# Two mixers after an attention stage on one core: normalisation issued earlier, transposes spread over units, five conversion steps instead of four

## The chip, the cores and the metric

The kernel runs on one core of a Trainium2 chip. The metric is the device time of one execution in microseconds (us). Engines are named as in the profile: PE is the matrix engine, DVE, ACT and POOL the vector, scalar and general engines, SP the one whose queue issues nearly all transfers (DMA).

## What is computed

The reference is a chain of three stages on a batch of 2, 768 positions and 512 channels. The first is attention with a window and block summaries, the second a mixer over tokens and channels, the third a normalised channel mixer. Cut to the last two, which matter here:

```
xt = x.transpose(0, 2, 1)
h = np.maximum(xt @ w_tok1, 0.0) @ w_tok2
u = x + h.transpose(0, 2, 1)
h2 = np.maximum(u @ w_ch1, 0.0) @ w_ch2
x = u + h2
...
mu = np.mean(x, axis=-1, keepdims=True)
var = np.mean((x - mu) ** 2, axis=-1, keepdims=True)
xn = (x - mu) / np.sqrt(var + 1e-06) * g_ln
ch = np.maximum(xn @ w_ch1, 0.0) @ w_ch2
return (x + ch).astype(np.float32)
```

The weights of both mixers arrive as 64-bit floats, the activations as 32-bit ones.

## The kernel before

Every product is made of three matmuls on pairs (high part, low part) of 32-bit numbers (`mm3`, L273 to L277). The activation `u` stays on the chip, 12 tiles of 128 positions by 512 channels; groups `g` 0 to 3 have three tiles each.

**Conversion of weights.** The 62 halves (128 by 512 each) of the weights are read as two 32-bit words per number, decoded on ACT (L115) and DVE (L129 to L137), and split into high and low part, on ACT (`split_hi`, `sp` or `slot`) and then DVE (`split_lo`). Halves 0 to 29 stay on the chip in `slot` tiles. Halves 30 to 61 are weights of the second mixer: they, and sums of their quarters (`sums`, tiles `sa`, `sb`, `sps`), are written back to DRAM (`w1s`, `w2s`) through two spill buffers `sp`, and are read again into a ring of 12 places as the second mixer needs them (`load_w1`, `load_w2`). The generator `conversion` (L141) cuts this work into steps: a step is about one DVE instruction with the ACT instruction and the transfers that belong to it. `convert_all(n)` issues n steps.

**First mixer.** After attention, 48 units each make one `g3` product and, one unit later, its `g4` accumulation (loop L925 to L972). Behind each unit stands `convert_all(4)` (L972). From unit 39 on the eight steps of `prep_x(0)` are issued between them, one a unit.

**prep_x.** `prep_x(s)` (L575) makes the operands of half `s` of the second mixer: eight steps, each for one 128-channel piece of one group. A step transposes three normalised 128 by 128 blocks on PE (tile `tx`, L585); then ACT evacuates them with the gain (`f`, L589), and ACT and DVE make and split the sums of pieces that the scheme of seven products needs (`split`, L569; T1 to T4). Its last act is to issue the normalisation of the next step (`normalize`, L549: three ACT instructions into the one tile `xn`). `start` runs a step up to its `yield`, the transposes; `finish` runs the rest.

**Second mixer.** 16 units (`unit`, L681), eight for each half `s`. A unit makes seven products of six matmuls (tile `m`, k = 0 to 6), each in one of two result banks of PSUM, which `tx` uses too; DVE adds them up (L686), except that ACT copies the first (tile `sm`, L696), and ACT and DVE make the relu pairs `ah`, `al` (L677, L678). Between the products stand the accumulations `acc_x` of the unit before (`second`, L733), three matmuls each, 12 a unit. After each product `step(k)` (L984) issues two or three conversion steps. In units 1 and 2, behind odd k, it also issues a step of the statistics of groups 2 and 3 (`norm_stats`, queued in `bg`, L993); what is left of them is issued at the end of unit 2 (L996). `prep_x(1)` follows at the ends of units 2 to 5, two of its steps at each (L999 to L1006).

**What sets the order.** PE's order in the second mixer is the one in which the code is written, ACT's from unit 10 of the first mixer on (manual schedule). DVE's and SP's orders are set by the scheduler when the program is built. Each engine takes its instructions in order.

Of the kernel before, what the change touches and what calls it, by code (L numbers as in the profile page):

```python
# [43 lines left out]
NP = F2 // 2  # L44
# [12 lines left out]
class Kern:  # L57
# [517 lines left out]
    def prep_x(self, s):  # L575
        nc = self.nc
        seq = [(e, half, i) for e in range(2) for half, i in ((0, 0), (0, 1), (1, 1), (1, 0))]
        self.normalize(2 * s + seq[0][2], seq[0][0] + 2 * seq[0][1])
        f, t = {}, {}
        for n, (e, half, i) in enumerate(seq):  # L580
            g, cc = 2 * s + i, e + 2 * half
            xn = self.xn.pop((g, cc))
            ps = self.ps_mm.tile([P, 512], F32, tag="mm", name=f"tx_{g}_{cc}")
            for j in range(GT):
                nc.tensor.transpose(ps[:, j * P : j * P + P], xn[:, j], self.ident)  # L585
            yield
            name = f"B{half + 1}{i + 1}"
            x = self.tmp.tile([P, GN], F32, tag="f", bufs=3, name=f"f{s}_{e}_{name}")
            nc.scalar.activation(x, ps[:, :GN], AF.Copy, scale=self.gt[:, cc : cc + 1])  # L589
            f[name] = x  # L590
            new = lambda k: self.tmp.tile([P, GN], F32, tag="t", bufs=2, name=f"t{s}_{e}_{k}")
            if name == "B12":
                t["T1"] = new("T1")
                nc.vector.tensor_tensor(t["T1"], x, f["B11"], op=ALU.subtract)
                self.split(s, "T1", e, t["T1"])
            else:
                self.split(s, name, e, x)
            if name == "B22":
                t["T3"], t["T2"] = new("T3"), new("T2")
                nc.vector.tensor_tensor(t["T3"], x, f["B12"], op=ALU.subtract)  # L600
                nc.vector.tensor_tensor(t["T2"], t["T3"], f["B11"], op=ALU.add)
                self.split(s, "T3", e, t["T3"])
                self.split(s, "T2", e, t["T2"])
            if name == "B21":
                t["T4"] = new("T4")
                nc.vector.tensor_tensor(t["T4"], x, t["T2"], op=ALU.subtract)
                self.split(s, "T4", e, t["T4"])
            if n + 1 < len(seq):
                e, half, i = seq[n + 1]
                self.normalize(2 * s + i, e + 2 * half)  # L610
            else:
                self.ready_xt.add(("x", s))
            yield

# [208 lines left out]
    def run(self):  # L823
# [100 lines left out]
        later = deque()  # L924
        for n, (s, f, g) in enumerate(units):  # L925
# [27 lines left out]
            if xctx is not None and not self.bg and not self.evacs:  # L953
# [15 lines left out]
                    {k: (at(f), 0) for f, k in enumerate(names)},  # L969
                    {k: (t, 0) for k, t in zip(names, flat + [at(f) for f in range(9, 12)])},  # L970
                ]
            self.convert_all(4)  # L972
        while later or self.bg or self.evacs:
            if later:
                self.bg.append(later.popleft())
# [6 lines left out]
        for n in range(2 * NP):  # L982

            def step(k):  # L984
                if n == 0 and k == 0:
                    for r in range(9, RING):
                        self.load_w1(r)
                self.convert_all(2 + k % 2)
                if n in (1, 2) and k % 2:
                    self.start(1)  # L990
                    self.finish()

            if n == 1:  # L993
                self.bg += [self.norm_stats(2)] * (GT + 1) + [self.norm_stats(3)] * (GT + 1)
            pending = self.unit(n, pending, step)
            while 0 < n < 3 and n == 2 and self.bg:  # L996
                self.start(1)
                self.finish()
            if n == 2:  # L999
                later += [self.prep_x(1)] * 8  # L1000
            if 2 <= n < NP - 1:
                for _ in range(2):
                    if later:
                        self.bg.append(later.popleft())
                        self.start(1)
                        self.finish()  # L1006
        while pending:
            pending.popleft()()

# [85 lines left out]
```

## Time and profile before

| what | us |
|---|---|
| runs (three): median, lowest, highest | 615.59, 613.78, 619.37 |
| the profiled execution's own time | 616.25 |
| its span, first to last instruction | 614.2 |
| PE busy | 572.8 |
| DVE busy | 413.2 |
| ACT busy | 257.9 |

The profile is of one execution; its times are us from the start of the span. A row of a timeline gives start, duration, engine, line, operation, tiles written and read, and in brackets the idle time of the engine before it with what ended it. Names in the profile leave out buffer numbers. Attention ends at about 105 us, the first mixer at 322, where unit 0 of the second begins.

### The profile page before, as it was taken

The numbers are of one execution on the slowest core, as the hardware profiler recorded it, in microseconds if no ns is written. First come the engines' busy times: TensorE is split into PE (matmuls) and PEld (weight loads), VectorE is DVE, ScalarE is ACT, GpSimd is POOL, SyncE is SP. The second block draws the span as 40 slices with busy tenths as digits, with TensorE's granted clock in tenths as the row PEclk, the third lists the DMA queues.
The fourth block names the chain that finished last, engine by engine and source line by source line (L and its number), as shares of the span: only waits on it lengthen the run. The fifth ranks groups of instructions, "written<-read, shape, count | busy, mean of one in ns | idle before, by whom it ended". The sixth has DMA issues, their size and how long they took to land.

```text
span 614.2 us, 9748 instructions
## 1 busy us (share of the span) xinstructions
PE 572.8 (93%) x3483; PEld 493.2 (80%) x3488; DVE 413.2 (67%) x992; ACT 257.9 (42%) x559; POOL 45.0 (7%) x78
## 2 busy tenths in 40 slices
PE   7777999999999999999998985798799999999997
PEld 3455778799998989998887874687689998899986
DVE  4699988992577986855798986876643543333334
ACT  4889887440334343325872335445411111111110
POOL 1565621000000000000000000000000000000000
PEclk9999999999999999999999996988999999999999
DMA  8999820442134354854579997875745776666412
GB/s 273 332 298 312 240 83 1 137 167 74 53 119 137 137 202 166 288 190 165 193 252 319 321 352 259 277 268 184 265 138 187 227 240 187 187 188 189 138 34 104
DMA packets 51206, 121.07 MB, mean 197 GB/s; under 512 B 5075, under 2 KB 11475, under 8 KB 51158
## 3 DMA queue, kind: packets, MB, share of 16 engines
q1 hardware_dynamic: 51152, 120.43, 60.3%
q8 instruction: 28, 0.46, 0.3%
q14 instruction: 20, 0.16, 0.1%
q10 hardware_dynamic: 6, 0.02, 0.0%
HBM read 94.21 MB, written 26.21 MB: 196 GB/s over the span
## 4 chain that ended last, share of the span: by engine, by line
PE 71%; DVE 11%; DMA 11%; ACT 4%; issue 2%; SPq 0%; ACTq 0%; DVEq 0%
PE acc_x L275 6%; PE acc_x L276 6%; PE acc_x L277 6%; PE m L275 5%; PE m L276 5%; PE m L277 5%; DMA stage<-in_wts_dram 3%; DMA w1s<-sps 3%; DMA V<-in_v_dram 2%; PE g L275 1%; DVE dec L133 1%; DMA VT<-in_vt_dram 1%; PE g L277 1%; PE g L276 1%; DVE dec L137 1%
## 5 line engine op out<-in xcount | busy, mean ns | idle before, releaser
L276 PE MATMUL acc_x<-slot,ah 128*128 128x512 f32 x192 | 77.0, 401 | 0.0
L275 PE MATMUL acc_x<-slot,ah 128*128 128x512 f32 x192 | 76.8, 400 | 0.0
L277 PE MATMUL acc_x<-slot,al 128*128 128x512 f32 x192 | 76.7, 400 | 0.0
L677 ACT ACTIVATE ah<-sm 128x384 fp32r<-128x384 f32 x32 | 16.7, 523 | 118.3 <-DVE sm L686 118.3
L275 PE MATMUL m<-slot,slot 128*128 128x384 f32 x126 | 45.0, 357 | 1.8 <-ACT sm L696 1.8
L137 DVE SCALAR_TENSOR_TENSOR dec<-stage,dec 128x512 uint32<-128x512 uint32 x62 | 44.1, 712 | 0.8
L115 ACT ACTIVATE dec<-stage 128x512 f32<-128x512 f32 x62 | 41.6, 675 | 5.9 <-DMA stage<-in_wts_dram 5.8
L133 DVE SCALAR_TENSOR_TENSOR dec<-stage,dec 128x512 uint32<-128x512 uint32 x62 | 43.4, 700 | 0.9
L276 PE MATMUL m<-slot,slot 128*128 128x384 f32 x126 | 44.0, 349 | 0.0
L277 PE MATMUL m<-slot,slot 128*128 128x384 f32 x126 | 43.9, 348 | 0.0
L277 PEld LDWEIGHTS acc_x<-slot,al 128*128 128x128 f32 x192 | 37.0, 193 | 8.4
L276 PEld LDWEIGHTS acc_x<-slot,ah 128*128 128x128 f32 x192 | 37.0, 193 | 4.2
L275 PEld LDWEIGHTS acc_x<-slot,ah 128*128 128x128 f32 x192 | 37.0, 193 | 3.9
L391 ACT ACTIVATE pr<-sn,mn 128x120 f32<-128x120 f32 x96 | 30.6, 386 | 6.6 <-DVE mn L381 6.3
L686 DVE TENSOR_TENSOR um<-m,sm 128x384 f32<-128x384 f32 x16 | 8.9, 557 | 30.7 <-PE m L277 30.7
L275 PEld LDWEIGHTS m<-slot,slot 128*128 128x128 f32 x126 | 24.8, 197 | 5.6 <-ACT sm L696 2.6
L131 DVE TENSOR_SCALAR dec<-dec 128x512 uint32<-128x512 uint32 x62 | 27.8, 449 | 0.6
L129 DVE TENSOR_SCALAR dec<-dec 128x512 f32<-128x512 f32 x62 | 26.3, 427 | 1.7 <-ACT dec L115 1.7
L678 DVE SCALAR_TENSOR_TENSOR al<-sm,ah 128x384 fp32r<-128x384 f32 x32 | 17.9, 558 | 13.9 <-ACT ah L677 13.9
L585 PE MATMUL tx<-ident,xn 128*128 128x128 f32 x48 | 12.1, 327 | 16.1 <-ACT xn L554 15.9
L276 PEld LDWEIGHTS m<-slot,slot 128*128 128x128 f32 x126 | 24.8, 197 | 2.2
L361 PE MATMUL scores<-K,Q 64*64 64x120 f32 x384 | 15.4, 275 | 10.2 <-DVE mn L381 7.5
(1392 smaller groups left out, 1486.2 us busy)
## 6 DMA issues: line engine op xcount, KB each, us to landing
stage<-in_wts_dram SPq DMA_DIRECT2D x62, 512.0 KB, 3.6
slot<-w1s SPq DMA_DIRECT2D x94, 256.0 KB, 3.4
slot<-w2s SPq DMA_DIRECT2D x32, 512.0 KB, 4.6
w1s<-sps SPq DMA_DIRECT2D x16, 512.0 KB, 3.8
w2s<-sp SPq DMA_DIRECT2D x16, 512.0 KB, 4.3
V<-in_v_dram SPq DMA_DIRECT2D x16, 306.0 KB, 7.6
extra<-w1s SPq DMA_DIRECT2D x18, 256.0 KB, 3.9
w1s<-sp SPq DMA_DIRECT2D x8, 512.0 KB, 5.2
```

Source lines behind the costliest of these rows:

```text
L115: nc.scalar.activation(m, self.raw[n][:, :, 1].bitcast(F32), AF.Abs)
L129: nc.vector.tensor_scalar(m, m, MAG_LO, MAG_HI, op0=ALU.max, op1=ALU.min)
L131: nc.vector.tensor_scalar(mi, mi, 3, 0x3FFFFFF8, op0=ALU.logical_shift_left, op1=ALU.bitwise_and)
L133: nc.vector.scalar_tensor_tensor(mi, t[:, :, 1], 0xC0000000, mi, op0=ALU.bitwise_and, op1=ALU.bitwise_or)
L137: nc.vector.scalar_tensor_tensor(mi, t[:, :, 0], 29, mi, op0=ALU.logical_shift_right, op1=ALU.bitwise_or)
L275: nc.tensor.matmul(out, lhs[0], rhs[0], start=first, stop=False)
L276: nc.tensor.matmul(out, lhs[0], rhs[1], start=False, stop=False)
L277: nc.tensor.matmul(out, lhs[1], rhs[0], start=False, stop=last)
L361: nc.tensor.matmul(ps[cols, j, e, :NK], Q[rows, 64 * w : 64 * w + 64], K.rearrange("p v c -> p (v c)")[rows, a : a + NK], start=True, stop ...
L391: nc.scalar.activation(pr[:, u], sn[:, u], AF.Exp, bias=mn[:, u : u + 1], scale=-1.0)
L677: nc.scalar.activation(ah, x, AF.Relu)
L678: nc.vector.scalar_tensor_tensor(al, x, 0.0, f32(ah), op0=ALU.max, op1=ALU.subtract)
```

## The change

Three things. In `prep_x` the normalisation of the next step is issued directly behind the evacuation `f`, ahead of the sums and splits. In the second mixer the statistics are all issued in unit 1, one step behind each product and two behind the last, and the eight steps of `prep_x(1)` are issued inside units 2 to 5, behind the products k = 1 and k = 5, instead of in pairs at the units' ends. And the first mixer issues five conversion steps behind each unit instead of four.

```
@@ prep_x @@
             nc.scalar.activation(x, ps[:, :GN], AF.Copy, scale=self.gt[:, cc : cc + 1])
             f[name] = x
+            if n + 1 < len(seq):
+                ne, nh, ni = seq[n + 1]
+                self.normalize(2 * s + ni, ne + 2 * nh)
             new = lambda k: self.tmp.tile([P, GN], F32, tag="t", bufs=2, name=f"t{s}_{e}_{k}")
...
-            if n + 1 < len(seq):
-                e, half, i = seq[n + 1]
-                self.normalize(2 * s + i, e + 2 * half)
-            else:
+            if n + 1 == len(seq):
                 self.ready_xt.add(("x", s))
             yield
@@ run @@
-            self.convert_all(4)
+            self.convert_all(5)
         while later or self.bg or self.evacs:
...
                 self.convert_all(2 + k % 2)
-                if n in (1, 2) and k % 2:
-                    self.start(1)
-                    self.finish()
+                if n == 1 or n in range(2, 6) and k in (1, 5):
+                    for _ in range(2 if (n, k) == (1, 6) else 1):
+                        self.start(1)
+                        self.finish()
 
             if n == 1:
                 self.bg += [self.norm_stats(2)] * (GT + 1) + [self.norm_stats(3)] * (GT + 1)
+            if n == 2:
+                self.bg += [self.prep_x(1)] * 8
             pending = self.unit(n, pending, step)
-            while 0 < n < 3 and n == 2 and self.bg:
-                self.start(1)
-                self.finish()
-            if n == 2:
-                later += [self.prep_x(1)] * 8
-            if 2 <= n < NP - 1:
-                for _ in range(2):
-                    if later:
-                        self.bg.append(later.popleft())
-                        self.start(1)
-                        self.finish()
```

PE's order at the end of unit 2 before the change. In the names the number behind `m` is the product k, the next the unit; behind `tx` stand the group and the channel piece.

```order
L277 MATMUL m6_2_4193<-slot9_1627,extra_1832 128x384
L275 MATMUL acc_x0_2_3891<-slot11_1825,ah_1_21_4019 128x512
L276 MATMUL acc_x0_2_3891<-slot11_1825,ah_1_21_4019 128x512
L277 MATMUL acc_x0_2_3891<-slot11_1825,al_1_21_4020 128x512
L585 MATMUL tx_2_0_4237<-ident_139,xn_2_0_4233 128x128 x3
L585 MATMUL tx_3_0_4249<-ident_139,xn_3_0_4245 128x128 x3
L275 MATMUL m0_3_4263<-slot3_1621,slot0_100 128x384
```

And with the change, around the first of those transposes, which now stands in the middle of unit 2:

```order
L277 MATMUL m1_2_4175<-slot7_1625,slot6_1624 128x384
L275 MATMUL acc_x0_2_3979<-slot11_1831,ah_1_11_4004 128x512
L276 MATMUL acc_x0_2_3979<-slot11_1831,ah_1_11_4004 128x512
L277 MATMUL acc_x0_2_3979<-slot11_1831,al_1_11_4005 128x512
L275 MATMUL acc_x0_3_3983<-slot11_1831,ah_1_12_4069 128x512
L276 MATMUL acc_x0_3_3983<-slot11_1831,ah_1_12_4069 128x512
L277 MATMUL acc_x0_3_3983<-slot11_1831,al_1_12_4070 128x512
L585 MATMUL tx_2_0_4203<-ident_139,xn_2_0_4199 128x128 x3
L275 MATMUL m2_2_4215<-slot8_1626,slot7_1625 128x384
```

The pair is apart: the first three transposes stand between the products 1 and 2 of unit 2, the second three (not shown) between its products 5 and 6.

ACT's order around the first two steps of `prep_x(1)` before, at the end of unit 2:

```order
L677 ACTIVATE ah_2_21_4202<-um_2_4061 128x384
L537 ACTIVATE sd_3_4219<-ve_3_4218 128x3
L554 ACTIVATE xn_2_0_4233<-u_137,nb_2_4089,rs_2_4081 128x128 x3
L589 ACTIVATE f1_0_B11_4241<-tx_2_0_4237,gt_140 128x384
L572 CAST xt0_67<-f1_0_B11_4241 128x384
L554 ACTIVATE xn_3_0_4245<-u_137,nb_3_4231,rs_3_4223 128x128 x3
L589 ACTIVATE f1_0_B12_4253<-tx_3_0_4249,gt_140 128x384
```

And with the change, in unit 2:

```order
L677 ACTIVATE ah_1_21_4123<-um_1_3977 128x384
L190 CAST sp57_4130<-dec57_3937 128x512
L115 ACTIVATE dec59_4132<-stage59_3963 128x512
L537 ACTIVATE sd_3_4139<-ve_3_4138 128x3
L696 COPY sm_2_4163<-m0_2_4155 128x384
L186 CAST sp58_4193<-dec58_4081 128x2x256
L115 ACTIVATE dec60_4195<-stage60_4108 128x512
L554 ACTIVATE xn_2_0_4199<-u_137,nb_2_4057,rs_2_4049 128x128 x3
L589 ACTIVATE f1_0_B11_4207<-tx_2_0_4203,gt_140 128x384
L554 ACTIVATE xn_3_0_4209<-u_137,nb_3_4151,rs_3_4143 128x128 x3
L572 CAST xt0_67<-f1_0_B11_4207 128x384
```

The second normalisation (`xn_3_0`) stands right behind the first evacuation `f`, and the first one stands behind the spill copy `sp58` and the magnitudes of half 60; before, conversion stood at halves 54 to 56 there.

## Rows read from the trace of the kernel before

**Rows 1.** The page: busy time and share of the engines, granted clock by slice, in tenths.

```profile
PE 572.8 (93%) x3483; PEld 493.2 (80%) x3488; DVE 413.2 (67%) x992; ACT 257.9 (42%) x559; POOL 45.0 (7%) x78
...
PEclk9999999999999999999999996988999999999999
```

**Rows 2.** PE's waits from 320 us on: in total, times, longest.

```profile
PE tx L585 <- ACT xn L554: 15.9, 5, 3.9
PE m L275 <- ACT sm L696: 1.8, 2, 1.2
```

**Rows 3.** PE's timeline: first products of units 2, 3, 7, 15, and around unit 2's end.

```profile
350.61 0.44 PE L275 MATMUL m<-slot,slot 128*128 128x384 f32 x1
...
372.00 1.25 PE L585 MATMUL tx<-ident,xn 128*128 128x128 f32 x3 [3.94 <-ACT xn L554]
...
377.28 0.67 PE L275 MATMUL m<-slot,slot 128*128 128x384 f32 x1
...
381.62 0.34 PE L275 MATMUL m<-slot,slot 128*128 128x384 f32 x1
...
384.06 0.34 PE L275 MATMUL m<-slot,slot 128*128 128x384 f32 x1
...
460.34 0.33 PE L275 MATMUL m<-slot,slot 128*128 128x384 f32 x1
...
586.02 0.34 PE L275 MATMUL m<-xt,slot 128*128 128x384 f32 x1
```

**Rows 4.** Three stretches: busy us (instructions) by engine, clock, transfer share, GB/s.

```profile
284.00:322.00 38.00, 37.79 (x198) 33.05 (x197) 31.15 (x65) 30.47 (x68) 0.00 (x0) 1.00 0.63 210
...
377.00:382.00 5.00, 5.00 (x17) 4.38 (x17) 1.45 (x3) 3.60 (x9) 0.00 (x0) 0.57 0.61 216
...
421.00:427.00 6.00, 5.94 (x23) 5.11 (x23) 2.12 (x5) 3.86 (x9) 0.00 (x0) 0.72 0.21 63
```

The engines are PE, PEld (weight loads), DVE, ACT, POOL in this order.

**Rows 5.** The transposes of the first mixer, 284 to 318: idle time before them.

```profile
  ACT xn L554: 0.2, 1
```

**Rows 6.** PE's timeline around one step in the first mixer.

```profile
288.01 0.40 PE L277 MATMUL acc_('u', 2)_0_2735<-slot,al_('u', 2)_12_3276 128*128 128x512 f32 x1
288.25 0.49 PE L585 MATMUL tx<-ident,xn 128*128 128x128 f32 x3
...
289.03 0.40 PE L277 MATMUL acc_('u', 2)_1_2736<-slot,al_('u', 2)_12_3276 128*128 128x512 f32 x1
289.27 0.39 PE L275 MATMUL acc_('u', 2)_2_2737<-slot,ah_('u', 2)_12_3275 128*128 128x512 f32 x1
```

**Rows 7.** ACT's timeline in unit 2.

```profile
355.93 0.62 ACT L250 CAST sps<-sb 128x512 fp32r<-128x512 f32 x1 [2.29 <-DMA w1s<-sp]
356.45 0.47 ACT L696 COPY sm<-m 128x384 f32<-128x384 f32 x1
...
366.08 0.62 ACT L190 CAST sp<-dec 128x512 fp32r<-128x512 f32 x1 [5.91 <-DMA w1s<-sps]
366.61 0.67 ACT L115 ACTIVATE dec<-stage 128x512 f32<-128x512 f32 x1
...
371.47 1.25 ACT L554 ACTIVATE xn<-u,nb,rs 128x128 f32<-128x128 f32 x3
```

**Rows 8.** DVE's timeline in unit 1: statistics among conversion.

```profile
342.33 0.18 DVE L527 BATCH_NORM_AGGREGATE mv<-st 128x2 f32<-128x6 f32 x1
342.43 0.67 DVE L526 BATCH_NORM_STATS2 st<-u 128x6 f32<-128x512 f32 x1
```

**Rows 9.** The page's groups: the costliest conversion instruction on DVE.

```profile
L137 DVE SCALAR_TENSOR_TENSOR dec<-stage,dec 128x512 uint32<-128x512 uint32 x62 | 44.1, 712 | 0.8
```

**Rows 10.** Waits of ACT for spill transfers, 320 to 450: in total, times, longest.

```profile
ACT sp L190 <- DMA w1s<-sps: 11.9, 3, 5.9
...
ACT sps L250 <- DMA w1s<-sp: 3.8, 3, 2.3
...
ACT sp L186 <- DMA w2s<-sp: 3.6, 2, 1.8
```

## Prediction

> **What bounds the kernel now.** I read the page's busy shares and slices first, then the waits of PE, then PE's timeline in the second mixer, then the stretches, and last what ACT and DVE do around the places found. PE is busy 93% of the span and its clock row shows 9 nearly throughout, with one dip [rows 1]. So the reader should not look for a slow engine, but for the stretch in which PE has holes. The list of PE's waits from 320 us on has one large entry: the transposes of `prep_x` waiting for the normalised tile `xn` from ACT, 15.9 us in 5 waits, the longest 3.9; the wait for the copy `sm`, 1.8 us, is far smaller [rows 2].
>
> PE's timeline shows the place [rows 3]. Behind unit 2's last accumulation PE stands idle 3.94 us before the first three transposes at 372.00, waits again before the next three, and starts unit 3's first product only at 377.28. That product and the six accumulations behind it take 377.28 to 381.62 = 4.34 us, the next such piece 381.62 to 384.06 = 2.44. The granted clock in 377 to 382 is 0.57, a stretch that lies mostly at 1.2 GHz, and 0.72 in 421 to 427 behind another such pause, against 1.00 in 284 to 322 [rows 4]. So each pause is paid twice: idle time, then a few us at half speed.
>
> The size of the whole follows from first products of units alone [rows 3]. Units 7 to 14 run from 460.34 to 586.02: 125.68 / 8 = 15.71 us each, PE's own pace. Units 2 to 6 run from 350.61 to 460.34 = 109.73 us; at that pace they would take 78.55. The excess is 31.2 us in five units, and four of their boundaries hold two transpose steps each.
>
> **The change part by part.** *Transposes one at a time, normalisation earlier.* The eight steps stay. Their cost where PE does not wait is seen in the first mixer, where such steps already lie among matmuls: from the accumulation at 288.01 over the three transposes at 288.25 to the third accumulation at 289.03 are 1.02 us, and plain accumulations are 0.24 apart (289.03 to 289.27), so three spacings would be 0.72: 0.30 us a step, 8 x 0.30 = 2.4 us [rows 6]. In that stretch PE waited for `xn` 0.2 us in all, once in eight steps [rows 5]. What can go is therefore 31.2 - 2.4 = 28.8 us: 15.9 waiting, the rest half-speed work and restarts.
>
> Does it go? For steps 2 to 8, yes: `xn` of the next step is now issued directly behind the evacuation `f` of the present one, ahead of the operand copies and sums, and the next transposes stand three or four products later. A product with its accumulations is 2.44 us [rows 3], so ACT has 7 us or more for the three normalisations, which take 1.25 [rows 7]. That is the cover; if ACT fell behind by more than it, the wait would be back. The normalisation delays the operand copies behind it by the same 1.25 us, and the operands are wanted first by unit 8, far off.
>
> *The first step has no such cover.* Its normalisation is issued after unit 2's second product, and its transposes are next in PE's order; behind them stands everything. ACT takes its instructions in order and was late there: before, the copy `sm` of unit 2's first product began at 356.45, behind a spill copy that waited 2.29 us for a transfer [rows 7]. Unit 2 began at 350.61, so PE is due at the transposes at 350.61 + 2 x 2.44 = 355.5. After the copy (ends 356.9) come a spill copy (0.62), the magnitudes of another half (0.67) and the first of the three normalisations (0.49 of the 1.25): 358.7, a wait of 3.2 us; the spill copy also waits for a decode that stands behind unit 2's first add on DVE, some 0.7 more. I take 4 us. The bounds are 0 (ACT on time, as in seven of the eight steps of the first mixer) and 3.2 + 5.9 = 9 (the spill copy ahead of `sm` meets a wait like the 5.91 at 366.08 [rows 7]). A pause of that length was followed by a slow piece, 4.34 - 2.44 = 1.9 us, so 2 more: 6 in all, bounds 0 and 11.
>
> *Statistics all in unit 1.* Counted in DVE's order from the first add of unit 0 to that of unit 1 there are now 29 instructions, before 26. The three more are one BN_STATS (0.67), one aggregation (0.10 to the next start) [rows 8] and one conversion instruction (0.71 at most [rows 9]): 1.5 us. From unit 1 to unit 2 the work on DVE is the same within 0.1 us, as conversion instructions make room for statistics. I assume no cover for it and put the 1.5 on the path; bounds 0 and 3.
>
> *Five conversion steps a unit in the first mixer.* By the program's order 291 steps are done when the second mixer begins, against 255, and the last decode moves from unit 5 to unit 2. A step costs DVE 0.71 us at most [rows 9]. In 284 to 322 DVE is busy 31.15 of 38 us [rows 4], so 9 units x 0.71 = 6.4 us just fit in the 6.85 free; PE has two result banks of slack. I put 1 us on the path for it, bounds 0 and 5. What it buys: units 3 to 5 lose nearly all decode and spill work, so from unit 4 on neither ACT nor DVE has more than PE's pace allows. With the steps their loads and spill stores move up in SP's queue, one load and one to two stores a half; they pass the ring loads of weights, which wait for PE there, and no wait of PE for a weight tile stands among its waits [rows 2].
>
> *Unit 3's spills.* The evacuation of the third step now stands behind the last spill copies, which wait for transfers: such waits cost ACT 11.9 us in three and 3.8 us in three [rows 10]. PE passes one product and its accumulations before it needs that bank, so of the longest (5.9) about 3 could reach it, of the others none. I take 2, bounds 0 and 5.
>
> **Sum.** 28.8 - 6 - 1.5 - 1 - 2 = 18.3 us. The profiled execution took 616.25 us, 0.66 above the median of the three runs (615.59), so 616.25 - 18.3 = 598.0, and from the median 597.3. I say 597.5. With all lower bounds taken the gain is 28.8 (587), with all upper ones 28.8 - 24 = 4.8 (611).
>
> **The rivals.**
> (a) *Everything goes.* The first step's `xn` is in time since transfers are fewer, and DVE's extra hides. For it: only tenths of waiting in the first mixer. Against: ACT's waits for transfers at 320 to 370, and the first step's missing cover. Gain 26 to 29, time about 588.
> (b) *ACT becomes the bound inside units 2 and 3.* The two result banks are now shared by products and transposes, so ACT's lateness stops PE at each of four steps: the first 9, the other three 2.3 each (as the 2.29 wait), and two slow pieces of 1.9: 20 us, with the 2.5 on DVE 22. Gain 28.8 - 22 = 7, time 609. For it: ACT's waits [rows 10]; against: the transfers ease, as 63 conversion steps remain for the second mixer, not 99.
> (c) *The slow side: the spills meet the first mixer.* The relu `ah` of the first mixer stands in ACT's order among spill copies. If a quarter more conversion brought the transfer waits of the second mixer there (11.9 + 3.8 + 3.6 = 19.3 us, over the 13 halves, 49 to 61, that the program's order has left for unit 0 and later, 1.5 a half [rows 10]), the 22 halves spilled before the second mixer would cost up to 33 us. It eats the gain from 18.3 / 22 = 0.8 us a half on; at the full price the time is 616.25 - 18.3 + 33 = 631. Against it: the transfer share in 284 to 322 is 0.63, and a quarter more conversion leaves it below 0.8.
> (d) *Each transpose step slows the matmuls behind it.* Eight slow pieces of 1.9 us are 15 us, which leaves a gain of 3, time 613. For it: the matmuls behind transposes were slow after the pauses (0.57). Against it: the eight steps of the first mixer lay among matmuls and the clock stayed at 1.00 [rows 4]. A rule of the Trainium skill is on its side: TensorE: Matmul & The Clock Gate, Part 4 (PE-mode transpose), says that full speed doesn't engage for transposes, as they don't count as PE work in the same way. By that rule, taken at its strongest, the time would be this rival's; the 1.00 does not agree, the 0.57 behind a pause does.
>
> **How the numbers follow.** The forecast (gain 13 to 23) has 0.60, (a) 0.16, (b) 0.15, (c) 0.04, (d) 0.05. A measurement of this kernel tells about 1% from no change, so faster means under 609.4: the forecast, (a) and two thirds of (b) = 0.86. Slower (over 621.7) is most of (c), 0.03; the rest, 0.11, is no change. The range 588 to 609 leaves out half of (a), a third of (b), (c) and (d): 0.08 + 0.05 + 0.04 + 0.05, a little over 0.2, so I carry its upper end to 610.
>
> **What would show it.** Right: PE's wait for `xn` falls from 15.9 to 3 to 6 us, nearly all of it at one place, some 5 us into unit 2; units 3 to 6 start 16 to 18 us apart, not 20 or more; the clock dips once. The first mixer stays without holes and unit 0 begins within 2 us of where it did. Wrong: several waits for `xn` or `f` in units 3 to 5 (rival b); holes of PE before 320 with ACT waiting for spill transfers (c); slow stretches around transposes without a pause (d); or unit 1 longer than 18 us, which would mean that the statistics cost more than 1.5.

## The result, and the profile after

The changed kernel takes 597.74 us (median of four runs), the kernel before 617.48 beside it; the ratio is 0.9675, 95% interval 0.9594 to 0.9757. One of the four runs took 1106.83 us; the ratio leaves it out, and the other three have a median of 596.93. The forecast was 597.5. The profiled execution took 596.65 us, its span is 594.5, against 616.25 and 614.2 before: 19.7 us less, where the sum had said 18.3.

The page of the changed kernel, busy share of PE and granted clock by slice (compare [rows 1]):

```profile
PE 569.3 (96%) x3488; PEld 491.6 (83%) x3488; DVE 407.8 (69%) x992; ACT 256.8 (43%) x559; POOL 44.2 (7%) x78
...
PEclk8998999999999999999999898999999999999999
```

PE does the same work in fewer us, so its share rises from 93% to 96%. The waits of PE from 320 us on, beside [rows 2]:

```profile
PE tx L585 <- ACT xn L554: 3.5, 1, 3.5
PE m L275 <- DVE um L686: 1.6, 2, 1.3
PE m L275 <- DVE sm L686: 1.2, 2, 0.9
PE m L275 <- ACT sm L696: 0.4, 1, 0.4
```

The large entry, 15.9 us in 5 waits for the normalised tile, has become one wait of 3.5. The waits for DVE's sums `um` and `sm`, 2.8 us in four, are not new but were fewer in the kernel before:

```profile
PE m L275 <- DVE sm L686: 1.3, 1, 1.3
PE m L275 <- DVE um L686: 0.5, 1, 0.5
```

PE's timeline says where each lies and what the units now take (beside [rows 3]):

```profile
334.21 0.49 PE L275 MATMUL m<-slot,extra 128*128 128x384 f32 x1 [1.35 <-DVE um L686]
...
338.73 0.44 PE L275 MATMUL m<-slot,extra 128*128 128x384 f32 x1 [0.27 <-DVE um L686]
...
352.81 0.33 PE L275 MATMUL m<-slot,slot 128*128 128x384 f32 x1
...
361.58 1.24 PE L585 MATMUL tx<-ident,xn 128*128 128x128 f32 x3 [3.53 <-ACT xn L554]
362.48 0.67 PE L275 MATMUL m<-slot,slot 128*128 128x384 f32 x1
...
363.27 0.52 PE L277 MATMUL m<-slot,slot 128*128 128x384 f32 x1
363.59 0.52 PE L275 MATMUL m<-slot,slot 128*128 128x384 f32 x1
...
366.24 0.34 PE L275 MATMUL m<-slot,slot 128*128 128x384 f32 x1
366.41 0.34 PE L276 MATMUL m<-slot,slot 128*128 128x384 f32 x1
...
372.86 0.49 PE L585 MATMUL tx<-ident,xn 128*128 128x128 f32 x3
...
373.44 0.44 PE L275 MATMUL m<-slot,extra 128*128 128x384 f32 x1
...
375.27 0.34 PE L275 MATMUL m<-slot,slot 128*128 128x384 f32 x1
...
380.15 0.49 PE L585 MATMUL tx<-ident,xn 128*128 128x128 f32 x3
380.39 0.42 PE L275 MATMUL m<-slot,slot 128*128 128x384 f32 x1
...
391.96 0.33 PE L275 MATMUL m<-slot,slot 128*128 128x384 f32 x1
...
441.12 0.33 PE L275 MATMUL m<-slot,slot 128*128 128x384 f32 x1
```

Unit 2 begins at 352.81, unit 3 at 375.27, unit 4 at 391.96, unit 7 at 441.12. So unit 3 takes 16.69 us, where it took 22.76; unit 2 is still long, 22.46. In it lies the one wait for `xn`, and behind that a slow piece: matmuls 0.32 apart at 363.27 and 0.17 at 366.24, half the clock. A wait of 1.35 stands at the start of unit 1, and behind it lies a second slow piece, the dearer one: the first product and its accumulations take 338.73 - 334.21 - 0.27 = 4.25 us for 2.44, so 1.8 too many, at a granted clock of 0.56. Five stretches of the changed kernel, columns as in [rows 4]:

```profile
318.00:333.00 15.00, 13.61 (x69) 11.80 (x67) 15.00 (x32) 6.05 (x11) 0.00 (x0) 1.00 0.93 322
333.00:349.00 16.00, 14.09 (x59) 11.99 (x60) 13.85 (x34) 4.61 (x9) 0.00 (x0) 0.89 0.93 309
...
334.20:338.10 3.90, 3.89 (x12) 3.44 (x12) 2.21 (x4) 1.60 (x3) 0.00 (x0) 0.56 0.90 320
...
349.00:365.00 16.00, 12.43 (x55) 10.47 (x55) 14.82 (x44) 9.41 (x21) 0.00 (x0) 0.90 0.93 331
...
375.00:442.00 67.00, 66.72 (x337) 59.46 (x337) 37.36 (x72) 26.87 (x60) 0.00 (x0) 1.00 0.65 206
```

From 375 to 442 PE is busy 66.72 of 67 us and the clock is 1.00, though six transpose steps lie there. Most of what is left to gain lies between 318 and 375. There DVE is busy 87 to 100% of the stretches shown, and the transfer engines are at a share of 0.93. ACT's timeline there (beside [rows 7]) shows what `xn` waited for:

```profile
349.31 0.62 ACT L250 CAST sps<-sb 128x512 fp32r<-128x512 f32 x1 [3.88 <-DMA w1s<-sp]
...
359.96 0.62 ACT L186 CAST sp<-dec 128x512 fp32r<-128x512 f32 x1 [1.59 <-DMA w2s<-sp]
...
361.05 1.25 ACT L554 ACTIVATE xn<-u,nb,rs 128x128 f32<-128x128 f32 x3
...
363.34 1.25 ACT L554 ACTIVATE xn<-u,nb,rs 128x128 f32<-128x128 f32 x3
```

ACT stands 3.88 us at a spill copy whose buffer is still being stored, later 1.59 at another, and the normalisation is behind it in ACT's order.

### The profile page after: what moved, and what is told of

The parts are those of the page before. It is cut to its first block, busy times and chain, and to the rows that moved or that the text cites. A ratio compares the mean times of both kernels' runs of the same rounds, so it can differ in the third digit from the quotient of the medians.

```text
span 594.5 us, 9756 instructions
## 1 busy us (share of the span) xinstructions
PE 569.3 (96%) x3488; PEld 491.6 (83%) x3488; DVE 407.8 (69%) x992; ACT 256.8 (43%) x559; POOL 44.2 (7%) x78
## 4 chain that ended last, share of the span: by engine, by line
PE 79%; DVE 7%; DMA 7%; ACT 5%; issue 1%; SPq 1%; ACTq 0%; DVEq 0%
PE acc_x L276 7%; PE acc_x L277 7%; PE acc_x L275 7%; PE m L275 6%; PE m L276 6%; PE m L277 6%; DMA stage<-in_wts_dram 4%; PE g L275 2%; DMA w2s<-sp 2%; PE g L277 2%; PE g L276 2%; ACT pr L391 2%; PE av L418 1%; DVE dec L133 1%; PE pt L398 1%
## 5 line engine op out<-in xcount | busy, mean ns | idle before, releaser
L276 PE MATMUL acc_x<-slot,ah 128*128 128x512 f32 x192 | 76.0, 396 | 0.0
L275 PE MATMUL acc_x<-slot,ah 128*128 128x512 f32 x192 | 75.9, 395 | 0.0
L677 ACT ACTIVATE ah<-sm 128x384 fp32r<-128x384 f32 x32 | 16.8, 524 | 109.4 <-DVE sm L686 109.4
L275 PE MATMUL m<-slot,slot 128*128 128x384 f32 x126 | 44.1, 350 | 1.1 <-ACT sm L696 0.4
L276 PE MATMUL m<-slot,slot 128*128 128x384 f32 x126 | 43.0, 342 | 0.0
L277 PE MATMUL m<-slot,slot 128*128 128x384 f32 x126 | 43.0, 341 | 0.0
L275 PEld LDWEIGHTS m<-slot,slot 128*128 128x128 f32 x126 | 24.0, 190 | 5.1 <-DVE um L686 1.3
L678 DVE SCALAR_TENSOR_TENSOR al<-sm,ah 128x384 fp32r<-128x384 f32 x32 | 17.8, 557 | 13.0 <-ACT ah L677 13.0
L131 DVE TENSOR_SCALAR dec<-dec 128x512 uint32<-128x512 uint32 x62 | 26.3, 424 | 0.4
L276 PEld LDWEIGHTS m<-slot,slot 128*128 128x128 f32 x126 | 24.0, 191 | 2.0
L361 PE MATMUL scores<-K,Q 64*64 64x120 f32 x384 | 16.4, 289 | 9.2 <-DVE mn L381 6.2
L686 DVE TENSOR_TENSOR sm<-m,sm 128x384 f32<-128x384 f32 x16 | 8.9, 555 | 23.3 <-PE m L277 23.3
```

The costliest lines, as they stand in the source:

```text
L131: nc.vector.tensor_scalar(mi, mi, 3, 0x3FFFFFF8, op0=ALU.logical_shift_left, op1=ALU.bitwise_and)
L275: nc.tensor.matmul(out, lhs[0], rhs[0], start=first, stop=False)
L276: nc.tensor.matmul(out, lhs[0], rhs[1], start=False, stop=False)
L277: nc.tensor.matmul(out, lhs[1], rhs[0], start=False, stop=last)
L677: nc.scalar.activation(ah, x, AF.Relu)
L678: nc.vector.scalar_tensor_tensor(al, x, 0.0, f32(ah), op0=ALU.max, op1=ALU.subtract)
```

## The experiments

Three theories stood against each other. **Distance:** a transpose step needs other work of PE between it and its normalisation; the change provides that. **Order in ACT:** what counts is that the normalisation goes ahead of sums and splits. **Crowding:** units 0 to 2 are late with either kernel, since conversion asks too much there, of DVE or of the two spill buffers and their transfers.

All twelve runs in one table. "Second mixer" is the end of the span less the start of unit 0 in the profiled execution: unit 0 began at 321.4 to 327.0 us in these executions, mostly because the first mixer itself began at 104.9 to 110.6; from there to unit 0 are 216.1 to 218.0 us in all of them, and PE had work in the whole of 260 to 300 us. So this length, though of one execution each, compares them more finely than the medians. The units' lengths are differences of first products in PE's timeline; "xn" is PE's wait for the normalised tile from 320 us on.

| kernel | median us | ratio to before (95%) | second mixer | units 0 to 5 | xn (times) |
|---|---|---|---|---|---|
| before | 617.48 | | 292.2 | 11.8 16.8 26.7 22.8 21.3 22.0 | 15.9 (5) |
| changed | 597.74 | 0.9675 (0.9594, 0.9757) | 273.1 | 12.8 18.6 22.5 16.7 16.7 16.7 | 3.5 (1) |
| before + normalisation early | 609.62 | 0.9864 (0.9834, 0.9894) | 285.0 | 13.5 16.5 25.0 20.7 20.0 19.8 | 9.7 (5) |
| before + five steps | 617.55 | 0.9999 (0.9980, 1.0019) | 291.3 | 13.9 17.6 24.8 21.6 21.0 22.0 | 15.0 (5) |
| before + spread | 600.39 | 0.9725 (0.9700, 0.9750) | 274.7 | 11.8 17.7 24.7 16.8 17.3 16.7 | 5.2 (1) |
| changed - five steps | 599.10 | 0.9701 (0.9656, 0.9746) | 274.1 | 13.5 17.0 23.9 16.8 17.0 16.7 | 4.1 (1) |
| changed - normalisation early | 601.21 | 0.9740 (0.9680, 0.9799) | 274.6 | 13.8 17.8 23.2 17.3 16.7 16.7 | 3.4 (1) |
| changed, first normalisation earlier | 595.13 | 0.9647 (0.9608, 0.9685) | 271.5 | 12.8 17.5 20.2 18.5 16.7 16.7 | 0 |
| changed, step at product 4 | 597.68 | 0.9679 (0.9632, 0.9726) | 273.1 | 12.8 17.5 24.2 16.4 16.4 16.6 | 4.9 (1) |
| changed, slow pace | 587.77 | 0.9513 (0.9466, 0.9560) | 262.1 | 10.3 15.8 16.7 16.7 16.7 16.7 | 0 |
| changed, light decode | 598.84 | 0.9682 (0.9617, 0.9746) | 274.0 | 11.3 18.0 24.7 17.4 16.7 16.7 | 4.8 (1) |
| before + slow pace | 618.13 | 1.0011 (0.9982, 1.0039) | 292.7 | 10.1 17.5 20.5 23.5 22.4 27.6 | 12.7 (5) |
| slow pace, step at product 4 | 586.48 | 0.9490 (0.9434, 0.9546) | 261.0 | 10.3 15.8 16.3 16.3 16.4 16.6 | 0 |
| the same, four steps | 606.50 | 0.9803 (0.9742, 0.9865) | 279.8 | 12.7 17.3 16.3 16.3 21.0 26.5 | 0 |

**The three parts, each alone.** First the normalisation only, on the kernel before:

```
@@ prep_x, the kernel before @@
             f[name] = x
+            if n + 1 < len(seq):
+                ne, nh, ni = seq[n + 1]
+                self.normalize(2 * s + ni, ne + 2 * nh)
...
-            if n + 1 < len(seq):
-                e, half, i = seq[n + 1]
-                self.normalize(2 * s + i, e + 2 * half)
-            else:
+            if n + 1 == len(seq):
```

> The kernel before with the earlier normalisation alone. My theory: the first step of prep_x(1) still waits 3.9 us, the second step of each pair waits only for the evacuation and its own normalisation, some 1.6 us instead of 3.1, 3.8, 1.8 and 3.3; so PE's wait for xn falls from 15.9 to about 10 us, the slow pieces stay, and the time falls by 5 us (3 to 8). Rival (the earlier normalisation is the cause of the gain): the wait falls below 5 us and the time by 15 or more.

Measured: 609.62, 1.4% less, and `xn` still waited for in the same five places, 9.7 us instead of 15.9. Those places are the first step and the second of each of the four pairs. The first step's wait falls from 3.94 to 2.55, that of the second step of the first pair does not (3.13, 3.23), and those of the other three fall from 3.76, 1.80 and 3.26 to 1.59, 1.25 and 1.10. That the time fell by 8 us where the wait fell by 6 fits a shorter stretch behind the last pair: unit 6 takes 15.8 us instead of 17.0.

Then the five steps only:

```
@@ run, the kernel before @@
-            self.convert_all(4)
+            self.convert_all(5)
```

> The kernel before with five conversion steps alone. My theory: the pairs at the units' ends stay and cost what they did; less spill work behind unit 3 lets the last two pairs come a little earlier. PE's wait for xn stays at 12 to 16 us, the time falls by 2 us (0 to 6). Rival (the transfers of the spills are what holds ACT, so moving them is the cause): the wait falls below 6 us and the time by 10 or more.

Nothing: ratio 0.9999. Emptying the later units of conversion doesn't help where pairs of transposes stop PE.

Then the spread only: the statistics in unit 1 and the transposes behind products 1 and 5, normalisation late, four steps:

```
@@ run, the kernel before: as in the change, without the fifth step and the part in prep_x @@
-                if n in (1, 2) and k % 2:
...
+                if n == 1 or n in range(2, 6) and k in (1, 5):
...
+            if n == 2:
+                self.bg += [self.prep_x(1)] * 8
```

> The statistics in unit 1 and the transposes one at a time inside units 2 to 5, but the normalisation at the end of a step as before and four conversion steps. My theory: distance alone removes the waits of steps 2 to 8, so PE waits for xn once, 3 to 6 us in unit 2, and the time falls by 14 us (10 to 18); with four steps the conversion runs to unit 5 and costs some us that the full change does not pay. Rival (each part gives a third): the time falls by 7 or less.

Measured: second mixer 17.5 us shorter of the 19.1 of the whole change. Of the five waits one is left, that of the first step:

```profile
PE tx L585 <- ACT xn L554: 5.2, 1, 5.2
```

So distance, not the order of the normalisation among sums and splits, carries the gain. This run moves the statistics too, and no run parts the two; that it is the transposes is read from the waits for `xn`.

**Each of the other two parts taken out of the change.** Four steps again:

```
@@ run @@
-            self.convert_all(5)
+            self.convert_all(4)
```

> The change without its fifth conversion step in the first mixer (four there, as before); the early normalisation and the spread transposes stay. Theory: the fifth step is worth 1 to 3 us beside the other two, since it empties units 3 to 5 of conversion; so this kernel is 1 to 3 us slower than the changed one, near 600, with unit 3 and unit 4 each 0.5 to 1.5 longer and with more waits of ACT for spill transfers in units 3 and 4. Rival: the distance alone carries everything and the fifth step is worth nothing, as it was on the kernel before (617.55 against 617.7): then within 0.7 us of the changed kernel.

```
@@ prep_x: the normalisation is back behind the sums and splits @@
-            if n + 1 < len(seq):
-                ne, nh, ni = seq[n + 1]
-                self.normalize(2 * s + ni, ne + 2 * nh)
```

> The change with the normalisation late again, behind the sums and splits; spread transposes and five steps stay. Theory: with three or four products between two steps the order inside ACT is indifferent, so units 3 to 6 stay at 16.7 and the time is within 1 us of the changed kernel. Rival: the late normalisation stands behind splits that wait for DVE, and unit 2 or 3 shows a second wait for the normalised tile of 1 to 3 us: 599 to 601.

The second mixer is 1.0 us longer without the fifth step and 1.5 without the early normalisation; the medians stand 1.4 and 3.5 above 597.74 (2.2 and 4.3 above 596.93), with intervals that overlap the changed kernel's. Without the fifth step units 3 and 4 are only 0.1 and 0.3 longer, less than expected. Without the early normalisation no second wait for `xn` appears, so the rival falls by its wait; but unit 3 is 0.6 longer, with one wait of 0.7 us for an evacuation, and the median is not within the theory's 1 us. These sizes are too small for the scatter to be settled.

**The first step's wait.** Its normalisation was issued in unit 2; here it goes behind the last product of unit 1:

```
@@ prep_x and run @@
-        self.normalize(2 * s + seq[0][2], seq[0][0] + 2 * seq[0][1])
+        (2 * s, 0) in self.xn or self.normalize(2 * s + seq[0][2], seq[0][0] + 2 * seq[0][1])
...
                 self.convert_all(2 + k % 2)
+                if (n, k) == (1, 6):
+                    self.normalize(2, 0)
```

> The full change, with the first normalisation of prep_x(1) issued behind unit 1's last product, ahead of that place's conversion steps, instead of in unit 2. My theory: the one wait of 3.5 us and the slow piece behind it (1.3 us) go but for about 1 us, in which the transposes wait for the bank that the late copy sm frees; the time is 3.5 us below the full change (2 to 5). Rival (the wait is only the first sign of ACT's lateness, and the next product waits in its place): less than 1 us.

The wait for `xn` is gone and unit 2 is 2.3 us shorter, but unit 3 is 1.8 longer; the second mixer gains 1.6, less than expected. PE's waits show what took its place, and the timelines of PE and ACT in unit 3 where:

```profile
PE m L275 <- DVE um L686: 3.3, 4, 1.4
PE m L275 <- ACT f_B L589: 2.1, 3, 1.1
```

```profile
389.33 0.45 PE L275 MATMUL m<-slot,slot 128*128 128x384 f32 x1 [1.08 <-ACT f_B L589]
...
381.86 0.62 ACT L190 CAST sp<-dec 128x512 fp32r<-128x512 f32 x1 [6.38 <-DMA w1s<-sps]
382.38 0.57 ACT L589 ACTIVATE f_B<-tx,gt 128x384 f32<-128x384 f32 x1
```

The evacuation of a transpose, whose bank the next product but one needs, stands behind a spill copy that waits 6.38 us for a transfer. DVE's split of that copy waits 2.77 us for it too, with sums behind it. PE loses little at once, and 1.08 us six us later; that this comes from the same wait is argued from the orders. PE comes to unit 3 2.5 us sooner than in the changed kernel; the spill copy does not (381.86 against 381.17).

**The pace of conversion.** One step fewer behind every product of the second mixer, 10 a unit instead of 17:

```
@@ run, step(k) @@
-                self.convert_all(2 + k % 2)
+                self.convert_all(1 + k % 2)
```

> The changed kernel with one conversion step fewer behind every product of the second mixer (one or two instead of two or three, 10 a unit instead of 17); the conversion of the last halves then ends in unit 6 instead of 4. Theory: what units 0, 1 and 2 still take above PE's pace (1 to 3, 2.9 and 5.7 us, with waits for the sums um, the copy sm and the normalised tile) is conversion work on DVE and ACT; seven steps fewer a unit are up to 7 x 0.7 = 4.9 us of DVE each, so unit 1 falls to 16 to 17.5 and unit 2 to 18 to 20, and the time by 3 to 6 us, to 591 to 594. Rival: these units wait for spill transfers or for their own chain of sums, whose length doesn't depend on the pace, and the conversion pushed into units 4 to 6 lengthens those: within 1 us of the changed kernel or up to 3 slower.

Ten us (11 in the second mixer), more than the theory's best: 587.77. Units 0 to 2 fall to 10.3, 15.8 and 16.7, and this is all that PE waits for from 320 us on:

```profile
PE m L275 <- DVE um L686: 0.4, 1, 0.4
```

The stretches speak against the reason in the expectation, though:

```profile
318.00:333.00 15.00, 14.58 (x75) 12.96 (x74) 15.00 (x32) 6.64 (x13) 0.00 (x0) 1.00 0.94 300
333.00:349.00 16.00, 16.00 (x81) 14.47 (x81) 15.66 (x43) 4.75 (x10) 0.00 (x0) 1.00 0.99 361
349.00:365.00 16.00, 15.90 (x83) 14.04 (x81) 12.47 (x33) 8.50 (x20) 0.00 (x0) 1.00 0.92 306
```

DVE is no less busy than before, 15.66 of 16 us in unit 1, and PE has no hole. So a DVE that is always busy does not stop PE by itself. By the profile's labels ACT differs: between 318 and 365 us none of its waits is put down to a spill transfer, where the changed kernel has 11.1 us in six (4.2, 4.0, 1.6 and 1.3 by kind). But three spill copies wait in this kernel as well, put down to DVE:

```profile
ACT sp L190 <- DVE um L686: 3.4, 1, 3.4
...
ACT sp L186 <- DVE dec L131: 2.4, 1, 2.4
ACT sp L188 <- DVE wm L686: 1.7, 1, 1.7
```

In a run below whose order is the same up to unit 2 (slow pace, step at product 4) the same copies wait as long and the label is a transfer. So it is not sure that these waits have another cause than before. What does differ is what stands behind them in ACT's order: here the copy `sm` of unit 1's first product comes ahead of the spill copy (334.67, then 337.52), in the changed kernel behind one (340.49, then 341.37).

**DVE's load alone taken away.** The pace stays, and the four decode instructions of the last ten halves work on 64 columns of 512; the others stay undecoded:

```
@@ decode @@
-        mi = m.bitcast(U32)
+        c = slice(0, 64 if h > 51 else 512); m = m[:, c]; t = t[:, c]; mi = m.bitcast(U32)
```

> The changed kernel at its own pace (17 conversion steps a unit, five in the first mixer), but the four decode instructions of DVE work on 64 of the 512 columns for halves 52 to 61, those decoded in the second mixer; the other columns stay undecoded, so the weights of the last products are others. Loads, spill stores, ACT's part and all splits and sums stay. What the four take of DVE falls from about 0.7, 0.7, 0.42 and 0.42 us to a fraction, some 1.5 to 2 us a half. Theory: units 0 to 2 are late because DVE has more work in them than PE; then this does what the slower pace did: unit 1 falls from 18.6 to under 16.5, unit 2 from 22.5 to under 19, and the time to 586 to 591, although as many bytes are stored in the same time. Rival: units 0 to 2 wait for the spill transfers, which take the two spill buffers and stop ACT; these come earlier still when DVE is faster, ACT's waits for transfers stay at 8 us or more, and the time stays at 594 or more.

The theory as I had put it falls. In units 1 and 2 DVE is busy 10.90 and 8.91 of 16 us,

```profile
333.00:349.00 16.00, 13.64 (x67) 11.68 (x66) 10.90 (x33) 5.62 (x12) 0.00 (x0) 1.00 0.96 351
349.00:365.00 16.00, 11.18 (x49) 9.45 (x49) 8.91 (x35) 8.05 (x18) 0.00 (x0) 0.87 0.84 304
```

and those units take 18.0 and 24.7 us, no less than with the full decode; only unit 0 is 1.5 shorter. ACT's timeline shows the chain whole: the spill copy waits 4.75 us for a store, the normalisation of the first step follows two instructions later,

```profile
360.18 0.62 ACT L186 CAST sp<-dec 128x512 fp32r<-128x512 f32 x1 [4.75 <-DMA w2s<-sp]
...
361.27 1.25 ACT L554 ACTIVATE xn<-u,nb,rs 128x128 f32<-128x128 f32 x3
```

and PE waits at its transposes as long:

```profile
361.80 1.25 PE L585 MATMUL tx<-ident,xn 128*128 128x128 f32 x3 [4.82 <-ACT xn L554]
```

So DVE's time alone is not what makes units 1 and 2 late. For unit 2's pause the cause is in these rows: a spill copy that waits for a store, with the first normalisation behind it in ACT's order. In this run unit 1 shows the same chain, with the copy `sm` in place of the normalisation:

```profile
339.50 0.40 ACT L188 CAST sp<-dec 128x256 fp32r<-128x256 f32 x1 [2.27 <-DMA w2s<-sp]
...
340.38 0.46 ACT L696 COPY sm<-m 128x384 f32<-128x384 f32 x1
...
340.89 0.44 PE L275 MATMUL m<-slot,slot 128*128 128x384 f32 x1 [1.94 <-ACT sm L696]
```

In the changed kernel that spill copy waits 1.25 us and PE 0.43; there most of unit 1's excess is the half-speed piece behind unit 0's pause. Unit 0 is DVE's for the most part: PE's waits for the sums in it fall from 2.6 us (0.35, 0.90, 1.35) to 0.7 (0.27, 0.41), and 1.5 of the 2.5 us go by which it is longer than with the slow pace. What the stores alone are worth is not shown: taking their waits away by themselves (a third spill buffer) was not tried.

**Slow pace without the change.** The same edit on the kernel before:

> The kernel before, with one conversion step fewer behind every product of the second mixer (10 a unit, not 17) and nothing else: pairs of transposes at the ends of units, late normalisation, four steps in the first mixer. Where the ring's loads need a half that isn't converted yet, its steps are issued at once there: some 2, 8 and 9 times two steps in units 3, 4 and 5. Theory: the pairs have no cover at any pace, so each of the four boundaries still shows a wait of 2 to 3 us for the normalised tile (8 to 12 in all) and units 2 to 5 stay at 19 or more; but units 0 to 2 lose their crowding as they do with the change: 605 to 611. Rival: what was late at the pairs was ACT and DVE under conversion work, so with less of it the waits for the normalised tile fall under 4 us and the time under 603, and the change's order was not needed. Third way: the heaped steps of units 3 to 5 cost more than the thinning brings, and the time is 615 or more.

Ratio 1.0011: the third way, by its time. Units 0 and 2 shorten, by 1.7 and 6.1 us, but PE still waits for `xn` five times, 12.7 us, and unit 5, where steps are issued in a heap, takes 27.6. The first part is the theory's: no pace gives a pair its cover. The edit that brings 10 us behind the change brings nothing ahead of it.

**The dearer place of the second step.** In the timeline above a product starts 0.58 us after the transposes behind product 5 (372.86, 373.44) and 0.24 behind product 1 (380.15, 380.39). So the step moves to product 4:

```
@@ run, step(k) @@
-                if n == 1 or n in range(2, 6) and k in (1, 5):
+                if n == 1 or n in range(2, 6) and k in (1, 4):
```

> The changed kernel with the second transpose step of units 2 to 5 behind the product 4 instead of the product 5. Theory: a step behind product 1 costs 0.33 us and one behind product 5 costs 0.67, since product 6 then needs the bank from which two sums of product 5 are still read, with one accumulation between; behind product 4 there are two accumulations and one sum, so four steps lose about 0.34 each: units 3 to 5 at 16.4 instead of 16.7 and the time 1.0 to 1.5 us lower. Rival: the cost is that of the transposes alone wherever they stand, and units 3 to 5 stay at 16.7.

Units 3 and 4 shorten by 0.34 and 0.37 us as expected, unit 5 by 0.08, but unit 2 is 1.7 longer, since the first `xn` came later (4.9 us). Unit 1, where the order is unchanged, is 1.1 shorter. The median does not move. With the slow pace, where nothing hides it, it is run again:

> The changed kernel with both edits: 10 conversion steps a unit in the second mixer, and the second transpose step behind product 4. Theory: with the pauses of units 0 to 2 gone, the cheaper place of the second step shows in the time: units 2 to 5 at 16.35 instead of 16.70, 1.0 to 1.4 us less than with the slow pace alone, near 586.5; this is the best kernel. Rival: the step behind product 4 finds ACT behind the relu of product 4 and brings a new wait for the normalised tile or for the evacuation: 588 or more.

586.48, and the second mixer 1.1 us shorter than with the slow pace alone, units 2 to 4 at 16.3 to 16.4. The medians differ by 1.3, within their scatter; unit by unit it is what was expected. ACT waits for spill transfers here too, 3.58, 2.09 and 1.35 us in units 0 and 1, and PE doesn't stop: such a wait harms only where something urgent stands close behind it. This is the fastest kernel of the study: 5.1% under the kernel before, and 1.9% under the changed one.

**What the fifth step buys.** That kernel with four steps in the first mixer:

> The same as the kernel with slow pace and the step behind product 4, but with four conversion steps a unit in the first mixer as before. The second mixer then begins 36 steps further back, and at 10 steps a unit the ring's loads overtake the conversion: 2, 8 and 9 times two steps are issued at once in units 3, 4 and 5. Theory: this is what the fifth step is worth, it buys the slow pace; the heaped steps are up to 16 x 0.6 = 10 us of DVE in one place of units 4 and 5 each, where PE has two banks of slack, so these units lengthen by 3 to 6 us each and the time is 593 to 599. Rival: DVE is idle for 40% of units 4 and 5 and takes the heap without PE noticing: within 1.5 us of the kernel with five steps, and the fifth step is worth nothing at any pace.

606.50: the fifth step, worth about nothing at the full pace, is worth some 19 us of the second mixer here. Units 2 and 3 are the same, but in units 4 and 5 the ring's loads ask for halves that aren't converted, the steps are issued in heaps, and PE stands behind DVE, whose sums come after the heap:

```profile
406.11 0.45 PE L275 MATMUL m<-slot,slot 128*128 128x384 f32 x1 [3.37 <-DVE sm L686]
...
432.42 0.69 PE L275 MATMUL m<-slot,slot 128*128 128x384 f32 x1 [8.64 <-DVE sm L686]
```

The heaps cost 4.7 and 9.9 us, more than the 3 to 6 each that I had expected. Units 0 and 1 are 2.4 and 1.5 longer as well, at the same pace; I didn't find out why.

## Why the prediction was right, and where it was not

**The place and the size.** Right: the excess of units 2 to 6. They took 109.73 us and take 441.12 - 352.81 = 88.31, so 21.4 less, where the sum had 28.8 - 6 - 2 = 20.8. Unit 2 begins 2.2 later, where it had 2.5 (statistics and fifth step). From unit 7 to the end 0.5 less, where it had nothing. In all 19.7 against 18.3.

**Steps 2 to 8 find their normalised tile in time.** Right, and for the reason given: no wait for them is left. The spread alone does it, though; issuing the normalisation ahead of sums and splits, half of my argument, is worth some 1.5 us of the second mixer beside it and 7 without it.

**A step costs 0.30 us.** Too small: units 3 to 5 take 16.7 against 15.7, 0.50 a step, 4.0 for eight where I had 2.4. Behind product 1 it is 0.33, behind product 5 0.67. My row was of the first mixer, where the next matmuls write other banks. Here product 6 comes right behind the transposes, one accumulation after product 5, and needs the bank of product 5, which is read by two sums. That reason is argued from the order; the run with the step behind product 4 shows 0.34 of it go.

**The first step.** The wait was to be 4 us and was 3.5, the slow piece 2 and was 366.24 - 362.48 - 2.44 = 1.3; together 4.8 for 6. My 1.9 had been read behind two waits, of 3.94 and 3.13 us. The reason, ACT late behind spill copies, was right.

**Statistics 1.5 and fifth step 1, by DVE's time.** The sum was nearly right and the reason wrong. The first mixer has no hole (PE 48.00 of 48 us from 270 to 318), and unit 0 began 0.6 us earlier, not later, so the fifth step cost nothing there. Units 0 and 1 grew by 1.0 and 1.8; unit 1 at 18.6 is longer than the 18 that I had named as the sign against me. The 1.8 is the size of the half-speed piece behind unit 0's pause: the clock, which I had let dip once, dipped twice. In the two runs with the same order up to there (first normalisation earlier, step at product 4) no such piece came, PE waited 1.19 and 1.32 us for `um` where it had waited 0.27, and unit 1 took 17.5; so some 1.1 us of the 18.6 is scatter. It is not DVE's time alone: with a fifth of it taken out of unit 1 (13.85 to 10.90 us) and two fifths out of unit 2 (14.82 to 8.91), unit 1 shortened by 0.6, less than that scatter, and unit 2 grew. The step that failed is "I assume no cover for it and put the 1.5 on the path": the count of DVE's instructions doesn't give the loss. What the runs show in its place: in unit 0 for the most part DVE's load; in unit 1 a half-speed piece behind a pause and waits for `um` and for a copy that stands behind a spill copy; in unit 2 ACT behind a spill store. That 2.5 came out near 2.2 is luck.

**Unit 3's spills, 2 us.** They cost nothing: ACT waited 3.8 there, and PE did not. The total is near partly since misses cancel: steps 1.6 dearer, the first step 1.2 and these spills 2 cheaper.

**The rivals.** (a) fell with the first step's wait. (b) happened in unit 2 alone; moving the first normalisation brought a piece of it into unit 3. (c) did not happen: in 284 to 322 the transfer share rose from 0.63 to 0.75 and PE was busy 38.00 of 38 us; the spills met units 0 to 2. (d) fell: six steps lie in 375 to 442 at a clock of 1.00, and the slow pieces stand behind pauses. The rule of the Trainium skill, TensorE: Matmul & The Clock Gate, Part 4 (PE-mode transpose), that full speed doesn't engage for transposes, is not borne out by steps of three transposes among matmuls, as that 1.00 shows.

**What I did not see.** That 10 us more lay in units 0 to 2 of the changed kernel, for one digit in the pace. I read the pace of conversion as given; it ran two to three units ahead of the ring's loads (in the changed kernel the last sums are stored from 378.1 us on, in unit 3, and their first load is issued at 415.1, in unit 5).

## What to carry to other kernels

A wait between two engines that comes back at each step of a chain goes when other work of the waiting engine stands between the steps; here the place of the normalisation in the other engine's order mattered less (7 us alone, against 17.5 for the distance). Background work needs only to meet its deadline: ask how far ahead it runs, and slow it where in-order engines carry both it and the critical chain, but not so far that its deadline issues it in heaps. An edit that is worth nothing alone (a fifth step, a slower pace) may be what another one needs, so try pairs before dropping one.

## What the runs showed of the hardware

A busy share near 1 is no bound by itself: DVE at 15.66 of 16 us left PE without a hole, and DVE at 8.91 of 16 stood beside PE at 11.18 of 16. Nor is the share of the transfer engines: 0.99 in the slow pace's unit 1 stood beside PE at 16.00 of 16 us, 0.93 in the changed kernel's beside 14.09.

The price of a pause is not fixed. Behind 3.53 us of waiting the matmuls ran 0.32 apart for about three us and cost 1.3 us more than at full clock; behind the 3.94 and 3.13 of the kernel before it was 1.9. In the changed kernel the waits of 0.35, 0.90 and 1.35 in unit 0 and at its end were followed by a piece that cost 1.8 (clock 0.56), and in the run with the step at product 4 waits of 0.35, 0.92 and 1.35 at the same matmuls by none:

```profile
335.94 0.44 PE L275 MATMUL m<-slot,extra 128*128 128x384 f32 x1 [1.35 <-DVE um L686]
...
333.00:349.00 16.00, 13.06 (x62) 11.09 (x63) 14.79 (x36) 5.15 (x10) 0.00 (x0) 1.00 0.97 334
```

The half-speed pieces stand behind pauses in these traces, but the length of a pause does not tell whether one follows or how long it is.
